# Strided sparse attention with a squared-ReLU feed-forward: v and w_in loads regrouped, v asked for later, and the seven-product form of the second matmul from the third block on

## The chip, the cores and the metric

The kernel runs on one core of one Trainium2 chip. The metric is the device time of one execution in microseconds (us), as the median of several runs; lower is better.

## What is computed

Two stages follow each other. Eight batches of eight heads go through a masked attention over 576 positions of 64 elements: the first four heads see the last 32 positions ("local"), the other four see positions at a distance that is a multiple of 32 ("strided"). The result, 4,608 tokens of 512 elements, goes through a feed-forward of width 2,048 with the activation s * relu(h)^2 + b.

```python
scores = scale * np.matmul(q, k.transpose(0, 1, 3, 2))
mask_local = (rel >= 0) & (rel < stride)
mask_strided = (rel >= 0) & (pos[None, :] % stride == pos[:, None] % stride)
attn = softmax(np.where(masks, scores, -1e9))
x = np.matmul(attn, v)            # (B, H, S, D) -> (B*S, H*D)
h = x @ w_in
g = s * (np.maximum(h, 0.0) ** 2) + b
out = g @ w_out
```

## The kernel before

**Work units.** A batch b is cut into four pairs of heads, m = 0 to 3 (0 and 1 local, 2 and 3 strided). `pair_steps` makes the steps of one pair: transposes of q and k (L429 for the local heads of batches 0 and 1, else L437), scores (L557; in batch 0 the mask is added by L554), exponentials on ACT (L575), a mask multiplication on DVE (L583), the product with v (L614, "AV"), the scaling by the reciprocal of the row sum (L629, then L640 on DVE or L635 on ACT), and a transpose of x into `xT` (L662). From some batch on, transposes of q, k and x are made by DMA on SP's queue instead: local k from batch 4, local q from batch 6, strided q and k from batch 3, local x from batch 2 and strided x in batches 4 to 6, the latter through DRAM (L685 writes, L689 reads back).

The feed-forward works on nine blocks T of 512 tokens. `ff1` (L907, "F1") makes h = x w_in in 16 column groups of four matmuls; ACT takes the ReLU out of PSUM (L934) and DVE or ACT squares it (L944, L942). `ff2` (L965, "F2") makes the second product for blocks 0 to 2: 64 matmuls of 512 columns each. `ff2_seven` makes it for blocks 3 to 8 as seven products in place of eight: 7 x 16 = 112 matmuls of 256 columns (L875), with sums of the activations (L747), differences of w_out's quarters (`w_mix`, L769, made once) and additions as the results leave PSUM (L794, L806, L817). The constant `SEVEN` is the first such block.

**What sets the order.** A planner (`Plan`) runs while the kernel is built. It keeps a clock of its own, an assumed cost for each step and an assumed delay for each result, and writes down one order per engine; on the chip every engine works its list in that order and waits on semaphores. `post` hands in work that is not PE's, with a cost per engine that may do it ("A" ACT, "V" DVE, "P" POOL, "D", "X", "Y" transfers on SP's queue); `flush` places it. `LAT` is the delay that is added after a cost, so an entry "D" is how long a DMA transpose is taken to need. `landing(cost)` is when a load on POOL's queue is taken to have landed. The main loop takes a step of the attention or a step of F1 or F2, whichever is due, and where nothing is ready in the head of the kernel, `keep_running` puts in a filler matmul (L1201).

**The loads.** Nearly all loads are issued by POOL. In the head: q and k of batch 0 in halves (L284), the strided q, k and v (L311), then, behind a copy that waits for qs, w_in in three pieces of 512, 512 and 1,024 columns (L328, in `weights_in`), then in `second` batch 1's q and k (L296), its v in four transfers, one a head (L316, rows of 64 elements), its strided v, w_out in four pieces (L334). Batch 0's local v comes through SP's queue in fp32 (L252, `stage_v`), into a part of w_out's tile, and POOL casts it. `rows_before` copies the 32 rows of v ahead of each band, `cast_v` casts strided v. Later batches: `fetch_qk(b + 2)` waits on POOL for batch b + 1's strided k transposes (copies into `gate`, L1036); `fetch_v(b + 2)` is posted when the last AV of batch b is placed.

In the built program POOL's transfers use eight semaphores in turn, and each transfer waits until the one eight before it has landed.

Of the kernel before, what the change touches and what calls it, by code (L numbers as in the profile page):

```python
# [15 lines left out]
class Plan:  # L16
# [7 lines left out]
    LAT = {"A": 70.0, "V": 70.0, "P": 70.0, "D": 12000.0, "X": 7000.0, "Y": 12000.0}  # L24
# [92 lines left out]
class Step:  # L117
    def __init__(self, fn, ns, needs=(), group=None, keys=(), posts=(), after=None):
        self.fn, self.ns, self.needs, self.group = fn, ns, needs, group
        self.keys, self.posts, self.after = keys, posts, after  # L120
# [3 lines left out]
def kernel(  # L124
# [32 lines left out]
    for p in range(SQ):  # L157
        for c in range(SQ):
# [30 lines left out]
               for i, n in enumerate((512, 512, 1024))]  # L189
# [21 lines left out]
    def x_free(b):  # L211
# [22 lines left out]
    vl_stage = w_out_sb.rearrange("p f m -> p (f m)").bitcast(FP32)[:, 0:NL].rearrange(  # L234
        "p (h t d) -> p h t d", h=4, d=D)
# [34 lines left out]
    for tl in p_bufs[False]:  # L270
        nc.vector.memset(tl[:, 16 * SQ:], 0.0)

# [40 lines left out]
    def load_vl(b):  # L313
        vl = v_loc[b % NV]
        for h in range(4):
            nc.gpsimd.dma_start(out=vl[LPAD:128, h, :, 0:D], in_=v_band(b, h))  # L316
# [8 lines left out]
    def load_w_in():  # L325
        wv = moe_w_in.rearrange("(c p) f -> p c f", p=128)
        for i, at in enumerate((0, 512, 1024)):
# [42 lines left out]
    def rows_before(b, mm, key):  # L370
# [3 lines left out]
        src = vl_stage[:, :, :, 0:D] if b == 0 else vl[:, :, :, 0:D]  # L374
# [3 lines left out]
        plan.post([key], {"P": 800.0} if b == 0 else {"A": 700.0, "V": 350.0}, g, [("in", "vl", b, mm)])  # L378
# [30 lines left out]
    def pair_steps(b, m):  # L409
# [10 lines left out]
        def trans(name, j, group):  # L420
            alone = loc and b < HEAD_T

            def f():
                if j == 0:
                    st["p" + name] = bank(group).bitcast(FP16)[:, 0:S]
                if alone:
                    for e in range(2):
# [12 lines left out]
            s = Step(f, 70 if alone else 35, needs=[("in", name + sfx, b, mm)],  # L440
                     group=group if j == 0 else None)
            if j == nt - 1:
# [35 lines left out]
        x_by_dma = b >= 2 if loc else XS_DMA <= b < B - 1  # L478
# [128 lines left out]
        def av(e, j, group):  # L607
# [13 lines left out]
            if j % per == per - 1:  # L621
# [10 lines left out]
                def mu(eng):  # L632
                    if eng == "A":
                        for i in range(per):
# [12 lines left out]
                                                 **({"A": 225.0 * per} if b == 0 else {})}, mu,  # L647
# [67 lines left out]
    SEVEN = 3  # L715
# [45 lines left out]
    def mix_post():  # L761
# [3 lines left out]
        jobs = ((3, wr[1], wr[0]), (1, wr[0], wl[0]), (2, wr[1], w_mix[1]), (4, wl[1], w_mix[2]))  # L765
        before = [("F2", SEVEN - 1)]
        for i, x, y in jobs:
            plan.post(before, {"V": 1250.0},
                      lambda eng, i=i, x=x, y=y: nc.vector.tensor_tensor(  # L769
                          out=w_mix[i], in0=x, in1=y, op=ALU.subtract), [("w_mix", i)])  # L770
            before = [("w_mix", i)]
# [125 lines left out]
    def ff1(T, ft, ct, group, cts=(0, 1, 2, 3), early=False):  # L897
        tok0 = T * PS
        def f():
# [6 lines left out]
            for lo, hi in ((0, n), (n, PS))[:1 + (n < PS)]:  # L906
                nc.tensor.matmul(  # L907
                    out=gts["h", T, ft][:, lo:hi],
                    lhsT=w_in_sb[min(ft // 4, 2)][:, ct].rearrange(
                        "p (c x l) -> p c l x", x=128, l=4)[:, max(ft // 4 - 2, 0), ft % 4],  # L910
# [111 lines left out]
    def landing(cost):  # L1022
# [4 lines left out]
        return ring + (6000.0 if plan.t > 60000.0 else 600.0)  # L1027
# [4 lines left out]
    def fetch_qk(b):  # L1032
# [6 lines left out]
        for name in ("q", "k"):  # L1039
# [3 lines left out]
            if b < HEAD_T:  # L1043
                arrive(both(name + "l", b), landing(1500))
                continue
            plan.done["raw", name, b] = landing(1700 if b > 1 else 1450)
            for mm in range(2):
                pair_post(b, name, mm, ("raw", name, b))
        for name in ("qs", "ks"):
            arrive(both(name, b), landing(2000 if b > 1 else 1750))  # L1050

    def fetch_v(b):
        load_vl(b)
# [9 lines left out]
    def early_v(b):  # L1063
# [3 lines left out]
        plan.done["raw", "v", False, b] = landing(1800)  # L1067
# [5 lines left out]
    def after_landing(i, src):  # L1073
# [3 lines left out]
    load_qk(0)  # L1077
    early_v(0)
    plan.free["P"] = 7100.0
    plan.free["V"] = 6500.0  # L1080
    AT = {"ql0": 5700.0, "kl0": 6800.0, "ql1": 7900.0, "kl1": 8900.0, "qs": 10100.0,
          "ks": 11600.0, "vs": 13600.0, "vl0": 7100.0, "vl1": 14700.0}
# [6 lines left out]
    stage_v(range(2, 4))  # L1089
# [3 lines left out]
    def weights_in(eng):  # L1093
# [4 lines left out]
        ring = 15300.0  # L1098
        for keys, cost in ([0], 2700), ([1], 2500), ([2, 3], 5000):
            arrive([("w_in", c) for c in keys], landing(cost))  # L1100

    for mm, at in (0, AT["vl0"]), (1, AT["vl1"]):
        plan.done["raw", "v", True, 0, mm] = at
        cast_v(0, True, mm, ("raw", "v", True, 0, mm))
# [7 lines left out]
    def second(eng):  # L1112
# [3 lines left out]
        plan.done["raw", "vl", 1] = landing(3200)  # L1116
# [5 lines left out]
    plan.post(both("vl", 0) + both("vs", 0) + [("w",)], {"P": 14000.0}, second, [("free",)])  # L1122
# [169 lines left out]
```

## Time and profile before

| | |
|---|---|
| median of 3 runs | 305.25 us (304.46 to 308.44) |
| the profiled execution: time, span | 306.2 us, 304.4 us |
| PE busy | 296.4 us (97%) |
| DVE, ACT, POOL busy | 216.6 (71%), 183.9 (60%), 99.3 us (33%) |
| POOL's DMA queue | 57,232 packets, 18.08 MB, 60.1% of 16 engines' span |
| SP's DMA queue | 43,562 packets, 18.78 MB, 33.3% |
| F1, 512 columns (L907) | 440 matmuls, 379 ns each |
| F2, 512 columns (L965) | 192 matmuls, 379 ns each |
| seven-product F2, 256 columns (L875) | 273 ns each |
| granted TensorE clock | 1.000 |

The span runs from the first to the last instruction of the profiled execution. A matmul's duration in the profile is longer than the distance from one start to the next, since matmuls are pipelined; for sums over a list of matmuls the distance is used. A slice of the busy rows is a fortieth of the span, 7.6 us.

### The profile page before, as it was taken

The numbers are of one execution on the slowest core, as the hardware profiler recorded it, in microseconds if no ns is written. First come the engines' busy times: TensorE is split into PE (matmuls) and PEld (weight loads), VectorE is DVE, ScalarE is ACT, GpSimd is POOL, SyncE is SP. The second block draws the span as 40 slices with busy tenths as digits, with TensorE's granted clock in tenths as the row PEclk, the third lists the DMA queues.
The fourth block names the chain that finished last, engine by engine and source line by source line (L and its number), as shares of the span: only waits on it lengthen the run. The fifth ranks groups of instructions, "written<-read, shape, count | busy, mean of one in ns | idle before, by whom it ended". The sixth has DMA issues, their size and how long they took to land.

```text
span 304.4 us, 6800 instructions
## 1 busy us (share of the span) xinstructions
PE 296.4 (97%) x2674; PEld 205.8 (68%) x2674; DVE 216.6 (71%) x474; ACT 183.9 (60%) x330; POOL 99.3 (33%) x146
## 2 busy tenths in 40 slices
PE   8998999999999999999999999999999999999995
PEld 3764655666555568767567776778888666766784
DVE  6665897698966688737997698777765366737563
ACT  2966963898747677478585946695725445445300
POOL 8771753930961095029502961200000000000000
PEclk9999999999999999999999999999999999999999
DMA  8999999999999699999999999944010200300123
GB/s 136 183 201 202 137 213 190 179 198 149 83 160 165 98 100 149 132 186 147 142 153 172 142 160 159 155 105 131 14 37 34 72 34 0 106 0 2 69 82 126
DMA packets 100826, 37.29 MB, mean 122 GB/s; under 512 B 80907, under 2 KB 97803, under 8 KB 100795
## 3 DMA queue, kind: packets, MB, share of 16 engines
q0 software_dynamic: 57232, 18.08, 60.1%
q1 hardware_dynamic: 43562, 18.78, 33.3%
q8 instruction: 21, 0.34, 0.5%
q14 instruction: 11, 0.08, 0.1%
HBM read 36.86 MB, written 10.32 MB: 155 GB/s over the span
## 4 chain that ended last, share of the span: by engine, by line
PE 83%; DMA 8%; DVE 3%; POOL 3%; issue 1%; ACT 1%; POOLq 0%
PE ps_f L907 36%; PE ps_f L875 20%; PE ps_f L965 12%; DMA kl<-in_k_dram 5%; PE ps_s L557 3%; PE ps_a L614 3%; DMA vs<-in_v_dram 2%; PE ps_s L875 2%; DMA xT<-x_dram 1%; PE ps_t L875 1%; PE ps_s L965 1%; PE ps_t L614 1%; PE ps_t L662 1%; PE ps_t L437 1%; PE ps_f L437 1%
## 5 line engine op out<-in xcount | busy, mean ns | idle before, releaser
L907 PE MATMUL ps_f<-xT,w_in_sb 128*128 128x512 f16 (+4 forms) x696 | 148.1, 340 | 0.0
L934 ACT ACTIVATE u<-ps_f 128x512 f16<-128x512 f32 x137 | 80.8, 595 | 72.6 <-PE ps_f L907 69.9
L907 PEld LDWEIGHTS <-w_in_sb 128*128 128x128 f16 x704 | 71.7, 113 | 33.1 <-DMA w_in_sb<-in_moe_w_in_dram 0.5
L875 PEld LDWEIGHTS <-gT 128*128 128x128 f16 x512 | 49.0, 98 | 12.5 <-issue 0.4
L965 PE MATMUL ps_f<-w_out_sb,gT 128*128 128x512 f16 x176 | 47.6, 379 | 0.0
L875 PE MATMUL ps_f<-w_out_sb,gT 128*128 128x256 f16 x312 | 44.2, 273 | 0.3 <-DVE o L806 0.3
L944 DVE TENSOR_TENSOR gT<-u 128x1024 f16<-128x1024 f16 x46 | 32.1, 697 | 15.1 <-ACT u L934 14.4
L942 ACT ACTIVATE gT<-u 128x1024 f16<-128x1024 f16 x26 | 27.5, 1057 | 0.7
L640 DVE TENSOR_TENSOR x_nat<-ps_a,rec 72x256 f16<-72x256 f32 (+1 forms) x55 | 25.3, 459 | 0.9
L316 POOL DMA_DIRECT2D v_loc<-in_v_dram x28 | 20.7, 759 | 14.3 <-DMA w_in_sb<-in_moe_w_in_dram 6.0
L965 PEld LDWEIGHTS <-gT 128*128 128x128 f16 x192 | 17.0, 98 | 11.1
L575 ACT ACTIVATE p_str<-ps_s 72x432 f16<-72x432 f32 (+1 forms) x45 | 20.1, 481 | 4.7 <-PE ps_s L557 4.6
L575 ACT ACTIVATE p_loc<-ps_s 128x384 f16<-128x384 f32 x46 | 20.8, 494 | 2.2 <-PE ps_s L557 1.8
L614 PEld LDWEIGHTS <-p_str 72*128 72x128 f16 x256 | 15.3, 98 | 7.3 <-issue 0.4
L747 DVE TENSOR_TENSOR gT<-gT 128x1024 f16<-128x1024 f16 x28 | 18.5, 683 | 1.4 <-ACT gT L942 1.3
L875 PE MATMUL ps_f<-w_mix,gT 128*128 128x256 f16 x144 | 19.3, 273 | 0.0
L875 PEld LDWEIGHTS <-S 128*128 128x128 f16 x160 | 15.5, 98 | 3.7
L629 DVE RECIPROCAL rec<-ps_a 72x4 f32<-72x4 f32 (+1 forms) x55 | 9.7, 177 | 11.2 <-PE ps_a L614 11.0
L321 POOL DMA_DIRECT2D v_str<-in_v_dram x16 | 13.0, 816 | 9.6 <-PE ps_f L907 5.6
L583 DVE TENSOR_TENSOR p_loc<-p_loc,masks 128x1152 f16<-128x1152 f16 x14 | 10.5, 750 | 7.6 <-ACT p_loc L575 7.4
L875 PE MATMUL ps_f<-w_mix,S 128*128 128x256 f16 x96 | 13.4, 273 | 0.0
L976 DVE SCALAR_TENSOR_TENSOR o<-ps_f,s_sb,bcs 128x512 f32<-128x512 f32 x11 | 8.2, 749 | 6.4 <-PE ps_f L965 6.2
(162 smaller groups left out, 413.2 us busy)
## 6 DMA issues: line engine op xcount, KB each, us to landing
out_dram<-o SPq DMA_DIRECT2D x34, 256.0 KB, 3.4
w_out_sb<-in_moe_w_out_dram POOLq DMA_DIRECT2D x4, 512.0 KB, 9.4
v_loc<-in_v_dram POOLq DMA_DIRECT2D x28, 72.0 KB, 8.5
qs<-in_q_dram POOLq DMA_DIRECT2D x6, 288.0 KB, 6.6
ks<-in_k_dram POOLq DMA_DIRECT2D x6, 288.0 KB, 8.0
ql<-in_q_dram POOLq DMA_DIRECT2D x5, 288.0 KB, 9.7
kl<-in_k_dram POOLq DMA_DIRECT2D x16, 72.0 KB, 3.8
v_str<-in_v_dram POOLq DMA_DIRECT2D x16, 72.0 KB, 9.9
```

The costliest lines, as they stand in the source:

```text
L316: nc.gpsimd.dma_start(out=vl[LPAD:128, h, :, 0:D], in_=v_band(b, h))
L321: nc.gpsimd.dma_start(out=vs[:, h, :, 0:D], in_=v[b, 4 + h].rearrange("(p j) d -> p j d", j=ST))
L575: nc.scalar.activation(out=st["pw", g][0:nk, 0:2 * n * nq], in_=st["s", g][0:nk, 0:2 * n * nq], func=AF.Exp, scale=scale)
L614: nc.tensor.matmul(out=st["a"][:, j % per, :], lhsT=st["pw", g][0:nk, i * nq:i * nq + WIDE], rhs=vt[0:nk, 2 * mm + e, j, :])
L640: nc.vector.tensor_tensor(out=st["x"][:, j0:j0 + per, 64 * e:64 * e + 64], in0=st["pa", e, j][0:nq, 0:per, 0:D], in1=st["rec", e, j][0:nq, ...
L747: nc.vector.tensor_tensor(out=at(out), in0=at(x), in1=at(y), op=op)
L875: nc.tensor.matmul(out=gts[name, T, t][:, 0] if halves else gts[name, T][:, t], lhsT=lhs(k, t), rhs=rhs(k), start=fresh and k == 0 and (ha ...
L907: nc.tensor.matmul(out=gts["h", T, ft][:, lo:hi], lhsT=w_in_sb[min(ft // 4, 2)][:, ct].rearrange("p (c x l) -> p c l x", x=128, l=4)[:, ma ...
L934: nc.scalar.activation(out=u, in_=gts["h", T, ft], func=AF.Relu)
L942: nc.scalar.activation(out=g, in_=u, func=AF.Square)
L944: nc.vector.tensor_tensor(out=g, in0=u, in1=u, op=ALU.mult)
L965: nc.tensor.matmul(out=gts[id_], lhsT=gts[T][:, ft, ts * 128:(ts + 1) * 128], rhs=w_out_sb[:, ft, cols], start=(ft == 0), stop=(ft == NFT ...
```

## The change

- Planner: a DMA transpose is taken to be ready after 8.0 us instead of 12.0 ("D"), a store to DRAM after 6.0 instead of 7.0 ("X"), a transposed read from there after 6.0 instead of 12.0 ("Y"); a late landing 3.0 us after the queue instead of 6.0. Several assumed landing times of the head change. The clock starts at 1.85 us.
- w_in is loaded in four pieces of 512 columns.
- Batch 0's second pair of local heads no longer comes through SP and a cast on POOL, but in one fp16-casting transfer on POOL's queue, ahead of the strided v. Batch 1's local v is one transfer instead of four.
- From batch 2 on `fetch_v(b + 2)` is placed only when all four `xT` of batch b are, and POOL first copies one element of each (`gate`), so it waits for them.
- x scalings may go to ACT in every batch, at 260 ns a group of 64 elements instead of 225 ns in batch 0 alone.
- Strided x of batch 7 goes through DRAM instead of PE's transposes.
- `SEVEN` is 2: block 2 has the seven-product form as well. w_mix 3, 2 and 4 are made after block 0's F2 and the bias sum, w_mix 1, which overwrites a part of w_out, after block 1's F2; w_mix 2 is made from w_mix 3.
- Once a transpose group of batch 0 is begun, its steps go first (`sticky`). Two small ranges of `p_str` are cleared.

```diff
-    LAT = {"A": 70.0, "V": 70.0, "P": 70.0, "D": 12000.0, "X": 7000.0, "Y": 12000.0}
+    LAT = {"A": 70.0, "V": 70.0, "P": 70.0, "D": 8000.0, "X": 6000.0, "Y": 6000.0}
...
-               for i, n in enumerate((512, 512, 1024))]
+               for i, n in enumerate((512, 512, 512, 512))]
...
     def load_vl(b):
         vl = v_loc[b % NV]
+        if b < 2:
+            nc.gpsimd.dma_start(
+                out=vl.rearrange("p h t d -> p (h t) d")[LPAD:128, :, 0:D],
+                in_=v.rearrange("b h (t p) d -> b p (h t) d", p=LQ)[b, :, 0:4 * LT])
+            return
         for h in range(4):
             nc.gpsimd.dma_start(out=vl[LPAD:128, h, :, 0:D], in_=v_band(b, h))
...
-        for i, at in enumerate((0, 512, 1024)):
+        for i, at in enumerate((0, 512, 1024, 1536)):
             nc.gpsimd.dma_start(out=w_in_sb[i], in_=wv[:, :, at:at + w_in_sb[i].shape[2]])
...
-        x_by_dma = b >= 2 if loc else XS_DMA <= b < B - 1
+        x_by_dma = b >= 2 if loc else XS_DMA <= b
...
-                                                 **({"A": 225.0 * per} if b == 0 else {})}, mu,
+                                                 "A": 260.0 * per}, mu,
...
-    SEVEN = 3
+    SEVEN = 2
...
-        jobs = ((3, wr[1], wr[0]), (1, wr[0], wl[0]), (2, wr[1], w_mix[1]), (4, wl[1], w_mix[2]))
-        before = [("F2", SEVEN - 1)]
-        for i, x, y in jobs:
-            plan.post(before, {"V": 1250.0},
+        early = [("bcs",)] + ([("F2", SEVEN - 2)] if SEVEN > 1 else [])
+        jobs = ((3, wr[1], wr[0], ALU.subtract, early), (2, w_mix[3], wl[0], ALU.add, []),
+                (4, wl[1], w_mix[2], ALU.subtract, []),
+                (1, wr[0], wl[0], ALU.subtract, [("F2", SEVEN - 1)]))
...
-        return ring + (6000.0 if plan.t > 60000.0 else 600.0)
+        return ring + (3000.0 if plan.t > 60000.0 else 600.0)
...
+    QUIET = 2
+
     def fetch_v(b):
+        for m in range(4) if b - 2 >= QUIET else ():
+
+            nc.gpsimd.tensor_copy(out=gate[0:1, m:m + 1], in_=x_slot(m, b - 2)[0:1, 0:1])
         load_vl(b)
...
     load_qk(0)
+    nc.gpsimd.dma_start(
+        out=v_loc[0].rearrange("p h t d -> p (h t) d")[LPAD:128, 2 * LT:4 * LT, 0:D],
+        in_=v.rearrange("b h (t p) d -> b p (h t) d", p=LQ)[0, :, 2 * LT:4 * LT])
     early_v(0)
...
-    stage_v(range(2, 4))
...
                 last_av.after = when_all("av", b, lambda b=b: plan.post(
-                    [("fetch", b + 2)] + both("vs", b), {"P": 3600.0}, lambda eng: fetch_v(b + 2),
-                    [("fetch_v", b + 2)]))
+                    [("fetch", b + 2)] + both("vs", b) +
+                    [("xT", b, mk) for mk in range(4) if b >= QUIET],
+                    {"P": 3600.0}, lambda eng: fetch_v(b + 2), [("fetch_v", b + 2)]))
...
+        active.sort(key=lambda p: not att[p][at_i[p]].sticky)
```

## The prediction

> **What bounds the kernel now.** I read the page's busy rows first, then the slices, the waits of PE, the timelines of PE and POOL in the head, and the chain.
>
> ```profile
> PE 296.4 (97%) x2674; PEld 205.8 (68%) x2674; DVE 216.6 (71%) x474; ACT 183.9 (60%) x330; POOL 99.3 (33%) x146
> ...
> PE   8998999999999999999999999999999999999995
> ...
> DMA  8999999999999699999999999944010200300123
> GB/s 136 183 201 202 137 213 190 179 198 149 83 160 165 98 100 149 132 186 147 142 153 172 142 160 159 155 105 131 14 37 34 72 34 0 106 0 2 69 82 126
> ```
>
> PE has no slice under 9 after the fourth, so from about 32 us on the kernel is its list of matmuls: an instruction taken off PE is time won, any other engine matters only if it makes PE wait. In the head PE's digits are 8 and 9 while DMA is at 9 from 8 us to past 100 us. The waits of PE, and its timeline there, say what for:
>
> ```profile
> PE ps_t L429 <- DMA ql<-in_q_dram: 1.4, 1, 1.4
> PE ps_t L429 <- DMA kl<-in_k_dram: 0.6, 1, 0.6
> ```
>
> ```profile
> 23.00 4.05 PE L907 MATMUL ps_f<-xT,w_in_sb 128*128 128x512 f16 x18
> 28.49 0.45 PE L429 MATMUL ps_t<-ident,ql 96*64 96x96 f16 x12 [1.44 <-DMA ql<-in_q_dram]
> 28.77 0.42 PE L429 MATMUL ps_f<-ident,ql 96*64 96x96 f16 x12
> 29.12 1.49 PE L907 MATMUL ps_f<-xT,w_in_sb 128*128 128x512 f16 x6
> 31.23 0.45 PE L429 MATMUL ps_t<-ident,kl 96*64 96x96 f16 x12 [0.62 <-DMA kl<-in_k_dram]
> ```
>
> PE has used up the w_in that it may use (18 F1 matmuls), then waits for batch 1's q and k. Those come when POOL's queue of transfers has come to them; POOL itself waits ahead of each v band:
>
> ```profile
> 22.06 0.75 POOL L316 DMA_DIRECT2D v_loc<-in_v_dram  x1 [1.96 <-DMA w_in_sb<-in_moe_w_in_dram]
> 26.89 0.72 POOL L316 DMA_DIRECT2D v_loc<-in_v_dram  x1 [4.08 <-DMA w_in_sb<-in_moe_w_in_dram]
> 28.73 0.73 POOL L316 DMA_DIRECT2D v_loc<-in_v_dram  x1 [1.11 <-DMA ql<-in_q_dram]
> 31.47 0.72 POOL L316 DMA_DIRECT2D v_loc<-in_v_dram  x1 [2.01 <-DMA kl<-in_k_dram]
> ```
>
> In the built program each POOL transfer waits for the one eight before it (eight semaphores in turn); these four waits fit that exactly. Two rows of the chain give the rates, and the DMA view of single issues two landings:
>
> ```profile
> 44.06 1.73 PE ps_f L965 x8
> ...
> 160.38 2.84 PE ps_f L875 x26
> ```
>
> ```profile
> w_out_sb<-in_moe_w_out_dram POOLq DMA_DIRECT2D x1, 512.0 KB, 6.5
> ```
>
> ```profile
> kT_alt<-kl SPq DMA_TRANSPOSE x1, 9.9
> ```
>
> A 512-column matmul costs 1.73/8 = 0.216 us, a 256-column one 2.84/26 = 0.109. w_out's first piece, issued at 33.63, lands at 33.63 + 6.5 = 40.1; the k transpose issued at 119.88 takes 9.9.
>
> **What the skill says.** "TensorE: Matmul & The Clock Gate", section Back-to-back issue gap: a warm matmul takes N/2.4 + 2.5 ns, so 215.8 and 109.2; the trace has 216 and 109. Halving the width thus costs 2 x 109 - 216 = 2 ns a pair. "DMA: Bandwidth & Descriptors", section Issuing engines are not separate DMA queues: SP's and POOL's transfers run on the same engines and interleave, so moving one from SP to POOL moves no load away. The trace agrees: 202 GB/s at a DMA share of 1.31 in 19.0 to 31.3 us. Same page, Why small descriptors are slow: short pieces pay overhead each. The trace: a window of 256-byte v rows (33.5 to 33.7) moved 78 GB/s, one of q, k and weights (35.5 to 36.4) 211. One v transfer in place of four still has 2,304 such rows, so I expect no faster landing.
>
> **Part 1, PE's list.** T = 2 goes to seven products. Out: 64 matmuls of 512 columns, 64 x 0.216 = 13.8 us. In: 7 x 16 = 112 of 256, 112 x 0.109 = 12.2. Net -1.6. Batch 7's strided x now goes through DRAM: 16 transposes L662 of 72 columns leave PE; four of them take 0.13 us from start to start in the timeline, so 16 x 0.032 = -0.5. Sum **-2.1 us**, certain. The fillers (20 before, 23 narrower ones after) only fill waits and count there.
>
> **Part 2, the head.** Counted in the two built orders. From the first F1 matmul (18.97) to kl's transposes, before has 38 F1; after has 45, and the other work done by then is equal (56 AV, 28 x transposes), because w_in's third piece is now 512 KB and counts as landed at half its way: the old 1 MB piece released POOL at 26.89, its predecessor at 22.06, so the new third lands near 24.5. Now 35 F1 (7.6 us), 12 AV (0.4), 16 transposes (0.5) and fillers (0.3) lie between first F1 and ql: 18.97 + 8.8 + 0.4 of small waits = 28.2, ql at 28.45: wait 0.25, not 1.44. Then 24 transposes and 10 F1, 0.8 + 2.2: 31.45, after kl (31.2): no wait. So seven F1 (1.5 us) more for 0.2 later: 1.3 won at 31 us. But from there to the first L965 lie 7.7 us of work: arrival 31.45 + 7.7 + 0.3 = 39.4, and w_out's first piece lands at 40.1 unless it moves. It cannot move much: bytes ahead of it are the same, and the engines are saturated, so POOL's earlier issue (no four waits of 2.0 + 4.1 + 1.1 + 2.0) only lengthens the queue. PE waits 0.7 there. Before, L965 began at 40.81 with 8 small scores (0.5 us) more done. Won: 40.8 - 40.1 - 0.5 = 0.2; I take **-0.4** (between 0 and -2: the upper end if SP's v rows, now on POOL's queue as fp16, leave w_in sooner). The second v half goes ahead of vs, w_in and all later POOL transfers: bounded by +1 (its rows delay w_in) and -1. POOL loses two casts and two v_str copies (3 us), hidden by w_in's landing at 18.9; the first ql at 5.2 instead of PE's 6.37 is hidden by it too. Without that cover it is worth 1.2.
>
> **Part 3, ACT.** The planner may now give any x scaling to ACT, at 260 ns an element group where it was 225 in batch 0 only. In the built order 76 of them stand on ACT, 12 before.
>
> ```profile
> L635 ACT ACTIVATE x_nat<-ps_f,rec x12: 307/330/362, 17.0 to 19.7; 72x64 f16<-72x64 f32 x12
> ```
>
> 64 x (333 - 260) = 4.7 us of ACT time that the plan doesn't know, in 14 blocks of about 0.3. ACT is at 60%, so most is absorbed; behind a block stands a relu L934 that frees an F1 bank, and PE waits for it if tight. Bounds 0 and +4.7; I take **+0.5**. DVE gains 8 sums (0.68), about 2 us of L794/L806, one add (0.69), loses 14 scalings (about 6): even. The four w_mix operations (1.2 us each) are as many as before and only stand earlier, behind T = 0 and T = 1; the first product that reads one comes 32 matmuls (3.5 us) into T = 2, long after. Four more small memsets (0.1 us each) and the order of batch 0's transposes lie ahead of w_in's landing: nothing.
>
> **Part 4, later v.** From batch 2 on four POOL copies wait for xT(b), then v(b+2). Behind them on POOL: eight v transfers (8 x 0.78), then the next q/k fetch and q copies. For v(4) xT(2) is complete at about 91 us; the gates (0.2 each) and two issues end at 93, landing 8.5 (page), copy 0.4 to 0.7: 102. Its first AV lies 11.7 us of PE work after xT(2)'s last transposes, near 103. Cover 1 us and more; for v(5) to v(7) it is over 5. **0**, at worst 1 each.
>
> **Part 5, plan latencies.** DMA-transposes are now planned at 8.0 us instead of 12.0 and landings at 3 instead of 6 beyond the ring. Batches 4 to 7 are therefore asked of PE up to 18 us earlier. Tightest: k(6,0). Its transpose stands on SP behind xT(5,0), which waits for F1 of T = 3; PE has 9.1 us of work between that issue and the first score. The trace has 4.3 in the median, 7.1 for kT_alt, 9.9 at most. Below nothing is excluded. **+0.2**, bounds 0 and +6.
>
> **Sum.** -2.1 - 0.4 + 0.5 + 0 + 0.2 = -1.8 us on the span: 304.4 to 302.6. The profiled execution took 306.2, 1.8 around the span, so 304.4; it lay 0.95 above the median. Against the median of 305.25: 303.45, say **303.5 us**.
>
> **Rivals.** (a) The head gives more: without SP's rows among POOL's, w_in and w_out land 1 to 2 us sooner, the 0.7 wait goes, the first-ql gain of 1.2 counts. For it: 2 us before w_in SP and POOL loads overlap. Against: the same rows remain. 2.5 us more: 301.0, reaching below 299.15 if the other 4 waits go as well. (b) Slower than before: SP's queue. kT(6,*) and kT(7,*) come late because their SP queue stands behind xT transposes held by F1, and land at 9.9 or more; every us beyond the cover of 9.1 is a PE wait, as PE runs in order. It decides from 2 us of lateness on; 3 to 5 us each in two batches give +6 to +10: about 310. Against: 4.3 median. (c) The change doesn't do what it says: the ACT blocks cost PE all that the seven products save, 2 us: 305.5.
>
> **Chances.** Forecast 0.50 (302 to 305), (a) 0.18, (b) 0.22, (c) 0.10. A third of (a) lies below 299.15 (-2%, about what a measurement of this kernel can tell from no change), a little over half of (b) above 311.35. So faster 0.06, same 0.82, slower 0.12. Range 300.5 to 309.5: it cuts the lower half of (a) and the upper half of (b).
>
> **What would show it.** Right: L875 at 784 matmuls of 109 ns and L965 at 128; PE's wait for kl gone, that for ql under 0.5, a new one of about 0.7 for w_out; PE at 9 from 40 us on. Wrong: PE waits for kT or qT between 125 and 185 us (b), for ACT L635 or L934 (c), for v_loc at 100 us (Part 4), or w_in's first landing away from 18.9 (a).

## The result and the profile after

The changed kernel took 316.06 us in the median of four runs (315.23 to 317.62), against 305.05 for the kernel before: a ratio of 1.0343, 95% interval 1.0258 to 1.0429. It is slower by about 11 us; the forecast of 303.5 and its range up to 309.5 missed it. The profiled execution took 316.18 us with a span of 314.4. (Ratios leave disturbed runs out, so they need not equal the quotient of two medians.)

After's line numbers are those of before plus 7 to 11: scores L565, AV L622, masks L591, ACT's and DVE's x scalings L643 and L648, F1 L918 with its ReLU L944, F2 L975, seven-product F2 L886, row copies L345, local v L323.

The page after: PE's busy time is almost that of before, but its slices now have 8s and 7s between 100 and 205 us, and the granted clock has a 7 in the slice that follows 133 us. DMA stays at 9 about as long as before.

```profile
PE 297.0 (94%) x2709; PEld 211.6 (67%) x2709; DVE 215.8 (69%) x476; ACT 197.5 (63%) x394; POOL 107.2 (34%) x157
...
PE   7989989999999899989997998799999999999994
...
PEclk9999999999999999979999999999999999999998
DMA  8999999996969999999999999923410300200223
```

PE's waits after (us in total, times, longest): the waits for batch 1's ql and kl, which led this list before, are gone. In their place stand three for the strided k transposes, three of over 1 us for DVE's results, and one for the very first ql.

```profile
PE ps_s L565 <- DMA kT<-ks: 6.2, 3, 2.2
PE ps_a L622 <- DVE p_loc L591: 1.6, 1, 1.6
PE ps_f L622 <- DVE p_loc L591: 1.2, 1, 1.2
PE ps_t L670 <- DVE x_nat L648: 1.2, 1, 1.2
PE ps_t L436 <- DMA ql<-in_q_dram: 1.1, 1, 1.1
```

PE's timeline after, in the stretch shown before: 21 F1 matmuls in a row, then ql and kl without a wait.

```profile
24.48 4.70 PE L918 MATMUL ps_f<-xT,w_in_sb 128*128 128x512 f16 x21
29.10 0.45 PE L436 MATMUL ps_t<-ident,ql 96*64 96x96 f16 x12
...
29.73 2.35 PE L918 MATMUL ps_f<-xT,w_in_sb 128*128 128x512 f16 x10
32.01 0.45 PE L436 MATMUL ps_t<-ident,kl 96*64 96x96 f16 x12
```

POOL's timeline after, in the stretch shown before: one v transfer where four stood, and w_out issued at 30.17 instead of 33.63.

```profile
23.93 1.19 POOL L318 DMA_DIRECT2D v_loc<-in_v_dram  x1 [2.31 <-DMA w_in_sb<-in_moe_w_in_dram]
...
30.17 0.55 POOL L341 DMA_DIRECT2D w_out_sb<-in_moe_w_out_dram  x1 [1.70 <-DMA kl<-in_k_dram]
```

The chain after (start, us, what): the two rates are unchanged, 1.08/5 = 0.216 and 2.07/19 = 0.109 us. But the chain now runs through a transpose of 8.93 us, and the seven-product matmuls behind it take 1.71/8 = 0.214 us each, half speed.

```profile
43.83 1.08 PE ps_f L975 x5
...
126.17 8.93 DMA kT<-ks
135.14 0.93 PE ps_s L565 x6
136.08 1.71 PE ps_f L886 x8
...
229.47 2.07 PE ps_f L886 x19
```

The DMA view (median us from issue to landing): the strided k transposes read 8.3 after, where the same row read 2.9 before. These medians stand on few transfers: of the eight transposes the trace has the landing of only two after (8.2 and 8.5) and three before (2.9, 2.9 and 4.4).

```profile
kT<-ks SPq DMA_TRANSPOSE x8, 8.3
```

I took PE's list of matmuls times the start-to-start distances of before (0.216, 0.109, 0.033 and so on) and compared it with the starts in the two traces. Before, the list makes about 290 us, and waits and half clock about 10. After, it is about 287 and 22. So the list became 2.8 us shorter (2.1 of it the steps of Part 1, the rest narrower fillers), and 12 us of waiting and half clock came in. Nearly all of it lies at 107, 133, 165, 194 and 199 us. At 107 us PE waits for an x scaling on DVE, which itself waited 2.28 us for a DMA transpose that reads x.

**At 133 us**, PE's timeline: after the F1 matmuls it waits 2.16 us for the transposed strided k of batch 5, issued by SP at 126.17.

```profile
131.72 1.26 PE L918 MATMUL ps_f<-xT,w_in_sb 128*128 128x192 f16 x10
135.14 0.93 PE L565 MATMUL ps_s<-qD_str,kT 128*72 128x144 f16 x6 [2.16 <-DMA kT<-ks]
135.87 1.92 PE L886 MATMUL ps_f<-w_mix,S 128*128 128x256 f16 x8
```

**At 165 us** PE waits for the strided k of batch 6. SP issues its transposes at 162.46, and PE has done the work ahead of them at 165.45, 3.0 us later; they come 5.1 us after the issue. This lead of the issue over the use is the cover of the transfer: 3.0 us where 5.1 were needed.

```profile
162.46 3.46 SPq L507 DMA_TRANSPOSE kT<-ks  x2
167.60 0.57 PE L565 MATMUL ps_s<-qD_str,kT 128*72 128x144 f16 x6 [2.15 <-DMA kT<-ks]
```

Before, SP issued the same two 1 us earlier, and PE came to them 11.3 us after that, without a wait:

```profile
161.47 3.10 SPq L499 DMA_TRANSPOSE kT<-ks  x2
172.78 0.54 PE L557 MATMUL ps_s<-qD_str,kT 128*72 128x144 f16 x6
```

**At 194 us**, three views tell one story. POOL's timeline: the copies that the change put ahead of v (L1067, the gates) come behind batch 7's q and k; the last of them waits for a transposed read of x, and v goes out at 178.77, where before it went out at 174.19.

```profile
169.09 2.95 POOL L295 DMA_DIRECT2D ql<-in_q_dram  x4
...
178.20 0.18 POOL L1067 COPY gate<-xT 1x1 f16<-1x1 f16 x1 [1.27 <-DMA xT<-x_dram]
178.77 2.92 POOL L323 DMA_DIRECT2D v_loc<-in_v_dram  x4 [0.40 <-PE ps_a L622]
```

DVE's timeline: its copy of v's preceding rows stands ahead of a mask multiplication and waits 3.87 us for the last v transfer, which lands at 193.8.

```profile
193.91 0.33 DVE L345 COPY v_loc<-v_loc 32x640 f16<-32x640 f16 x1 [3.87 <-DMA v_loc<-in_v_dram]
194.26 0.69 DVE L954 TENSOR_TENSOR gT<-u 128x1024 f16<-128x1024 f16 x1
194.87 0.75 DVE L591 TENSOR_TENSOR p_loc<-p_loc,masks 128x1152 f16<-128x1152 f16 x1
```

PE then waits 1.56 us for that mask (L622, the second row of its waits). Before, the same row copy on DVE waited for nothing: v had landed at 184.6, 9 us earlier.

```profile
193.61 0.33 DVE L338 COPY v_loc<-v_loc 32x640 f16<-32x640 f16 x1
```

### The profile page after: what moved, and what is told of

The parts are those of the page before. It is cut to its first block, busy times and chain, and to the rows that moved or that the text cites. A ratio compares the mean times of both kernels' runs of the same rounds, so it can differ in the third digit from the quotient of the medians.

```text
span 314.4 us, 6974 instructions
## 1 busy us (share of the span) xinstructions
PE 297.0 (94%) x2709; PEld 211.6 (67%) x2709; DVE 215.8 (69%) x476; ACT 197.5 (63%) x394; POOL 107.2 (34%) x157
## 4 chain that ended last, share of the span: by engine, by line
PE 77%; DMA 16%; DVE 3%; issue 2%; ACT 1%; SPq 0%; POOL 0%; POOLq 0%; DVEq 0%
PE ps_f L918 31%; PE ps_f L886 20%; PE ps_f L975 7%; DMA kT<-ks 6%; PE ps_s L565 4%; DMA v_loc<-in_v_dram 4%; DMA xT<-x_dram 2%; DMA xT<-x_nat 2%; PE ps_a L622 2%; PE ps_s L886 2%; DMA ql<-in_q_dram 1%; PE ps_t L886 1%; PE ps_s L975 1%; PE ps_t L444 1%; DVE x_nat L648 1%
## 5 line engine op out<-in xcount | busy, mean ns | idle before, releaser
L918 PE MATMUL ps_f<-xT,w_in_sb 128*128 128x512 f16 (+4 forms) x696 | 149.4, 340 | 0.2 <-DVE x_nat L648 0.2
L944 ACT ACTIVATE u<-ps_f 128x512 f16<-128x512 f32 x137 | 80.9, 597 | 58.3 <-PE ps_f L918 57.4
L918 PEld LDWEIGHTS <-w_in_sb 128*128 128x128 f16 x704 | 72.2, 113 | 29.5
L886 PEld LDWEIGHTS <-gT 128*128 128x128 f16 x608 | 57.8, 98 | 13.8 <-ACT gT L952 0.3
L886 PE MATMUL ps_f<-w_out_sb,gT 128*128 128x256 f16 x376 | 53.0, 272 | 0.1
L954 DVE TENSOR_TENSOR gT<-u 128x1024 f16<-128x1024 f16 x45 | 30.7, 685 | 19.4 <-ACT u L944 18.9
L975 PE MATMUL ps_f<-w_out_sb,gT 128*128 128x512 f16 x112 | 29.7, 379 | 0.0
L755 DVE TENSOR_TENSOR gT<-gT 128x1024 f16<-128x1024 f16 x34 | 22.6, 680 | 1.6 <-ACT gT L952 1.4
L886 PE MATMUL ps_f<-w_mix,gT 128*128 128x256 f16 x176 | 22.9, 273 | 0.0
L886 PEld LDWEIGHTS <-S 128*128 128x128 f16 x176 | 17.6, 101 | 4.4
L648 DVE TENSOR_TENSOR x_nat<-ps_a,rec 72x256 f16<-72x256 f32 (+1 forms) x42 | 19.4, 462 | 0.6
L323 POOL DMA_DIRECT2D v_loc<-in_v_dram x24 | 17.6, 745 | 4.9 <-DMA w_out_sb<-in_moe_w_out_dram 3.4
L622 PEld LDWEIGHTS <-p_str 72*128 72x128 f16 x256 | 15.1, 98 | 5.7 <-issue 0.3
L886 PE MATMUL ps_f<-w_mix,S 128*128 128x256 f16 x112 | 17.0, 285 | 0.0
L975 PEld LDWEIGHTS <-gT 128*128 128x128 f16 x128 | 11.5, 98 | 7.8
L345 POOL COPY qD_str<-qT 64x576 f16<-64x576 f16 x6 | 5.2, 864 | 33.5 <-DMA qT<-qs 24.7
L622 PEld LDWEIGHTS <-p_loc 128*128 128x128 f16 x192 | 9.4, 98 | 6.8 <-DVE p_loc L591 3.3
```

Source lines behind the costliest of these rows:

```text
L622: nc.tensor.matmul(out=st["a"][:, j % per, :], lhsT=st["pw", g][0:nk, i * nq:i * nq + WIDE], rhs=vt[0:nk, 2 * mm + e, j, :])
L648: nc.vector.tensor_tensor(out=st["x"][:, j0:j0 + per, 64 * e:64 * e + 64], in0=st["pa", e, j][0:nq, 0:per, 0:D], in1=st["rec", e, j][0:nq, ...
L755: nc.vector.tensor_tensor(out=at(out), in0=at(x), in1=at(y), op=op)
L886: nc.tensor.matmul(out=gts[name, T, t][:, 0] if halves else gts[name, T][:, t], lhsT=lhs(k, t), rhs=rhs(k), start=fresh and k == 0 and (ha ...
L918: nc.tensor.matmul(out=gts["h", T, ft][:, lo:hi], lhsT=w_in_sb[ft // 4][:, ct].rearrange("p (x l) -> p l x", l=4)[:, ft % 4], rhs=xT[ct][: ...
L944: nc.scalar.activation(out=u, in_=gts["h", T, ft], func=AF.Relu)
```

## Experiments

Theory 1: the planner's shorter assumed delays ask PE for transposes and loads before they have landed. Theory 2: the gates hold back later loads. Theory 3: the seven-product block 2 itself. The times of the kernel before beside these runs were 305.7 to 306.2 us.

### Undoing the two parts in the changed kernel

```diff
-    LAT = {... "D": 8000.0, "X": 6000.0, "Y": 6000.0}
+    LAT = {... "D": 12000.0, "X": 7000.0, "Y": 12000.0}
-        return ring + (3000.0 if plan.t > 60000.0 else 600.0)
+        return ring + (6000.0 if plan.t > 60000.0 else 600.0)
```

> The changed kernel with the planner's assumed delays of before: a DMA transpose 12.0 us again, the way through DRAM 7.0 and 12.0, a late landing 6.0 after the queue; the rest of the change stays. Theory 1 (the shorter assumed delays ask PE for strided k of batches 5, 6 and 7 before it has landed): the three waits for kT<-ks (2.33, 2.31 and 2.02 us) and the 1.2 us at half clock behind the first go, so about 308 us. Theory 2 (the copies that hold back the later v hold back everything behind them on POOL): no gate is touched, so at least the v_loc wait of 1.7 and the kT wait of 2.0 in batch 7 stay, 312 us or more. Theory 3 (neither: the seven-product form of block 2 itself costs the time): stays at 316.

Measured: 312.91 us, 1.0217 (1.0145 to 1.0289).

```diff
-    QUIET = 2
+    QUIET = 100
```

> The changed kernel with v of batches 4 to 7 fetched as before (no wait for xT(b), no copies ahead of it); the short assumed delays stay. Theory 1: kT<-ks waits of batches 5 and 6 stay; at most the v_loc wait of 1.7 us and the 2.0 us behind it in batch 7 go, so 312 to 314 us. Theory 2: the transfers of the later batches start earlier and land before they are asked for, all of the 10 us of waits after 100 us shrink, 308 or less. Theory 3: 316.

Measured: 311.78 us, 1.0222 (1.0160 to 1.0283). Then both edits together:

> The changed kernel with both undone: old assumed delays, no gates. What stays of the change is the head's loads, the seven-product form of block 2, ACT scalings in all batches, batch 7's strided x through DRAM. Theories 1 and 2 together: no wait over 1 us after 60 us but those of DVE, about 304.5 (the net of my working of the list, -2.1, against 305.05 and the two DVE waits of 1.3 and the late DMA x wait). Theory 3: over 311.

Measured: 305.43 us, 0.9993 (0.9975 to 1.0011).

The two parts are the whole loss: without both, the time is that of before. Either one left in costs about 7 us (2.2 to 2.3% of 305.7), so they overlap: together 10.6, not 14. Theory 3 falls as the main cause. With both undone no wait of PE for a transfer over 0.84 us is left. Each theory is right about its own waits: with long delays PE no longer waits for k at all, and without the gates one such wait (2.64 us) and one for DVE (2.39) stay.

With the delays long and the gates in, the loss sits at one place. ACT's timeline of that run: two row copies wait for v in turn, 4.38 and 3.49 us, and the ReLU that frees F1's bank stands behind them.

```profile
189.48 0.58 ACT L944 ACTIVATE u<-ps_f 128x512 f16<-128x512 f32 x1
194.44 0.73 ACT L345 COPY v_loc<-v_loc 32x640 f16<-32x640 f16 x1 [4.38 <-DMA v_loc<-in_v_dram]
198.66 0.72 ACT L345 COPY v_loc<-v_loc 32x640 f16<-32x640 f16 x1 [3.49 <-DMA v_loc<-in_v_dram]
199.29 0.58 ACT L944 ACTIVATE u<-ps_f 128x512 f16<-128x512 f32 x1
```

PE's timeline of the same run: it waits 5.87 us for that ReLU, and then its F1 matmuls come every 0.42 us instead of 0.216.

```profile
199.92 1.87 PE L918 MATMUL ps_f<-xT,w_in_sb 128*128 128x512 f16 x4 [5.87 <-ACT u L944]
```

### One part alone on the kernel before

Only the four delays, as in the change:

> The kernel before with only the planner's assumed delays of the change (8.0, 6.0 and 6.0 us; late landing 3.0). Against the changed kernel without gates, which lies 6.4 us over the one with both undone, this asks if the short delays need the rest of the change to do harm. Theory 1 alone: they do not, about 311 us with PE waiting over 2 us for kT<-ks or a transposed q or k twice. Rival (the head, the faster block 2 or batch 7's x through DRAM crowd SP's queue, the delays only show it): 306 to 307.

Measured: 317.9 us, 1.0359 (1.0278 to 1.0439), even more than the whole change. PE's waits in that run, first two rows:

```profile
PE ps_s L557 <- DMA kT<-ks: 3.6, 1, 3.6
PE ps_f L907 <- ACT u L934: 3.0, 1, 3.0
```

The second is once more an engine held by a copy: ACT's copy of batch 6's transposed q waited 6.16 us for its DMA with a ReLU behind it. Theory 1 needs nothing else of the change. The rival (the delays only show a crowded queue) falls. What the delays did can be counted in the cover of the strided k of batches 4 to 7: 12.6, 12.5, 11.3 and 7.8 us in the kernel before, 7.7, 5.4, 6.1 and 5.2 in this run.

Only the gates:

```diff
     def fetch_v(b):
+        for m in range(4) if b - 2 >= QUIET else ():
+            nc.gpsimd.tensor_copy(out=gate[0:1, m:m + 1], in_=x_slot(m, b - 2)[0:1, 0:1])
...
-                    [("fetch", b + 2)] + both("vs", b), {"P": 3600.0}, lambda eng: fetch_v(b + 2),
+                    [("fetch", b + 2)] + both("vs", b) +
+                    [("xT", b, mk) for mk in range(4) if b >= QUIET],
+                    {"P": 3600.0}, lambda eng: fetch_v(b + 2),
```

> The kernel before with only the later v (v of batches 4 to 7 asked for behind xT of two batches earlier, with the copies on POOL). Theory 2 alone: the last v lands 10 to 14 us after its issue at about 182, its row copy stands on ACT or DVE before a relu or a mask, PE waits 5 us or more near 190: about 312. Rival (the gates harm only a kernel that is asked for v early): 306 to 307.

Measured: 305.58 us, 0.9984 (0.9963 to 1.0005). My expectation was wrong, the rival right: alone, the gates cost nothing.

Only `SEVEN = 2` with its order of w_mix:

> The kernel before with the seven-product form from block 2 on and nothing else (with the w_mix order of the change). Theory 1 and 2: the 64 matmuls of 512 columns become 112 of 256, -1.6 us of PE and no new wait: 303.5 us. Theory 3: the change of pace or DVE's sums bring waits: 306 or more.

Measured: 304.81 us, 0.9980 (0.9956 to 1.0004). No loss, but a gain of only 0.6 us (0.2%), where the list gives 1.6, and the interval takes in no gain at all.

The seven-product block and the gates together:

> The kernel before with the seven-product form from block 2 on and the gates, nothing else. Theory A: ACT is not loaded more, so about 305. Theory B: the faster block takes the cover, PE waits for v of batch 7 or behind it: 310 or more.

Measured: 308.6 us, 1.0072 (1.0046 to 1.0098). That is 2.8 us more than the block alone, so Theory A falls; of Theory B the direction is right and not the size (310 or more). Only one wait in that run stands behind the last v: 1.07 us at 195.5, for a ReLU behind a row copy on ACT that waited 2.29. PE's other new waits over 0.9 us are for DVE (1.65 and 0.98), and its clock was at half from 17.6 to 21.1 us. In POOL's queue v of batch 4 goes out at 94.0, as in the changed kernel with long delays (94.1), where the gates alone on the kernel before let it out at 89.9 and without gates it goes at 83 to 84. At 89.9 the later fetches catch up (v of batch 7 at 174.9, before 174.2); at 94 they don't (178.5, and 182.2 in the changed kernel with long delays).

ACT's scalings, a suspect for the late gate, put back in the changed kernel with long delays and gates:

```diff
-                                         "A": 260.0 * per}, mu,
+                                         **({"A": 225.0 * per} if b == 0 else {})}, mu,
```

> The changed kernel with the long assumed delays and with x scalings on ACT only in batch 0, as before; the gates stay. With ACT's scalings this lay at 312.9, the gates alone on the kernel before cost nothing (305.6). Theory A (ACT, busy with scalings, copies xT(2) 4 us later, at 93.4 instead of 89.2, and so opens the gate of v(4) later; every later fetch then starts later): the gates open early again, POOL's first v of batch 7 goes out near 175, about 306. Theory B (it is the faster pace of block 2 and the head that leave the gates no cover): near 312.

Measured: 310.91 us, 1.0137 (1.0091 to 1.0183), v of batch 7 out at 182.3. Theory A falls: the fetches are as late as with the scalings.

### Which delay, and how much of it

In the changed kernel without gates, only the transposes' delays short:

> The changed kernel without gates, the assumed late landing back at 6.0 us, the transposes' delays short (8.0, 6.0, 6.0). Theory 1a (the transposes' delay is what is asked too early): near 311, as with both short, with PE waiting 2 us for kT. Theory 1b (the landing's delay is): 305.5, as with both long.

Measured: 309.97 us, 1.0068 (1.0037 to 1.0099), with times that spread from 305.8 to 313.2, between the two theories. Only the landing short:

> The changed kernel without gates, the transposes' delays back at 12.0, 7.0 and 12.0, the assumed late landing short (3.0 us). Theory 1a: 305.5. Theory 1b: near 311.

Measured: 314.38 us, 1.0287 (1.0213 to 1.0361). The landing, which covers the loads of q, k and v, is the dearer one. The two don't add up: both short gave 1.0222.

Then the kernel before with delays half way, and with longer ones:

```diff
-    LAT = {... "D": 12000.0, "X": 7000.0, "Y": 12000.0}     ... 6000.0 if plan.t
+    LAT = {... "D": 10000.0, "X": 6500.0, "Y": 9000.0}      ... 4500.0 if plan.t
+    LAT = {... "D": 18000.0, "X": 10000.0, "Y": 18000.0}    ... 9000.0 if plan.t
```

> The kernel before with assumed delays half way to the change: 10.0, 6.5 and 9.0 us, late landing 4.5. Cover theory: the last v's row copy, which has 8.8 us of cover with the long delays and waits 2.6 us with the short ones, still has some 2 to 4 us: no transfer wait over 1 us, 305 to 309. Rival (any new plan moves the time, whatever the delays): 310 or more.

Measured: 311.02 us, 1.0115 (1.0038 to 1.0192). It lies between short and own delays, but I expected no transfer wait over 1 us, and there are two causes of that size: 1.3 us for kT, and 2.5 us behind a row copy that sat 3.2 us on ACT. The time is the one that the rival named, and this run doesn't exclude it: its own waits are for transfers, but it may be that almost any other order than the kernel's own costs something.

> The kernel before with longer assumed delays: 18.0, 10.0 and 18.0 us, late landing 9.0. As in the changed kernel with these delays: no wait for a transfer after 60 us, cover of 12 us or more, but attention runs out later, F2's seven-product blocks wait for DVE's evictions 4 to 7 us in all: 309 to 312. If longer is simply safer: 305 to 306.

Measured: 316.79 us, 1.0316 (1.0249 to 1.0384), above what I expected. PE's waits in that run: no transfer after 60 us, but DVE's results at several places. PE's clock was also at half from 155.4 to 162.2 us, around two of these waits. That longer delays cost almost as much as short ones fits the rival of the run before; what shows the short delays' own part is which waits come with them.

```profile
PE ps_a L614 <- DVE x_nat L640: 2.2, 2, 1.6
PE ps_f L875 <- DVE Va L794: 1.5, 3, 0.9
...
PE ps_f L875 <- DVE w_mix L769: 1.3, 1, 1.3
```

The changed kernel, gates and all, with these longer delays:

> The changed kernel, gates and all, with assumed delays longer than before's: 18.0, 10.0 and 18.0 us, late landing 9.0. If the gates cost because the plan leaves too little cover between the fetch and the work that reads it, the 5.9 us behind the last v's row copy go and this lies at 306 to 308 (with 12.0 and 6.0 it was 312.9). If POOL's chain of fetches is the bound, waits only change their place: 312 or more.

Measured: 312.37 us, 1.0203 (1.0183 to 1.0224). Neither reading holds as I wrote it. The waits for transfers do go (v lands at 193.4 and is asked for at 208.2), so the cover was what the gates ate, and POOL's chain is not the bound. But the time does not fall, since other waits come:

```profile
PE ps_f L886 <- DVE Va L805: 3.3, 5, 0.8
PE ps_f L886 <- DVE Vb L805: 1.9, 3, 0.8
```

Attention is asked for later; the seven-product blocks then wait for DVE to empty their banks, eight times 0.25 to 0.84 us.

Side by side, the last v load of all runs: when it is issued, how many of SP's transposes are issued while it is under way, how long it takes to land, when it has landed, and when the engine has come to the second of the two row copies that read it. "Long" delays are those of before, "old ACT" is ACT scalings in batch 0 alone; the last part below has the runs that were not named yet.

| run | v(7) issued | transposes meanwhile | to landing | landed | second copy reached |
|---|---|---|---|---|---|
| changed, longer delays | 184.4 | 4 | 9.0 | 193.4 | 208.4 |
| before, gates | 174.9 | 4 | 9.7 | 184.5 | 192.1 |
| before | 174.2 | 3 | 10.4 | 184.6 | 193.6 |
| before, longer delays | 181.8 | 1 | 10.5 | 192.3 | 204.3 |
| changed, both undone, old ACT | 174.8 | 5 | 11.8 | 186.6 | 190.6 |
| changed, both undone | 172.4 | 5 | 12.6 | 185.0 | 188.7 |
| before, block 2 and batch 7's x, ACT at 333 | 175.7 | 6 | 14.5 | 190.2 | 193.1 |
| before, block 2 | 172.7 | 4 | 14.6 | 187.3 | 189.0 |
| changed | 178.8 | 6 | 15.0 | 193.8 | 190.0 |
| before, head | 176.1 | 6 | 15.1 | 191.2 | 193.3 |
| before, block 2 and gates | 178.5 | 6 | 15.2 | 193.7 | 191.5 |
| before, short delays | 175.1 | 7 | 15.7 | 190.9 | 188.3 |
| changed, no gates | 172.3 | 7 | 16.0 | 188.3 | 187.9 |
| before, half-way delays | 177.3 | 6 | 16.4 | 193.7 | 190.6 |
| changed, long delays | 182.2 | 7 | 16.4 | 198.6 | 195.2 |
| changed, long delays, old ACT | 182.3 | 7 | 16.5 | 198.8 | 196.1 |
| before, block 2 and batch 7's x | 172.7 | 5 | 17.7 | 190.4 | 188.9 |
| before, block 2 and batch 7's x, ACT at 260 | 175.6 | 7 | 18.5 | 194.0 | 193.3 |
| changed, no gates, transposes' delays long | 167.9 | 8 | 19.2 | 187.1 | 183.3 |
| changed, no gates, landing's delay long | 175.7 | 5 | 19.3 | 195.0 | 198.6 |

The same load takes 9.0 to 19.3 us, and the delays don't decide it: with the delays of before and no gates it runs from 10.4 to 18.5. Nor is it shown that the transposes do. Runs with six and more of them lie at 14.5 to 19.2, but those with five at 11.8 to 19.3, block 2 alone has four and 14.6, and a load that takes longer leaves time for more. The Trainium skill says ("DMA: Bandwidth & Descriptors", Issuing engines are not separate DMA queues) that transfers from SP and POOL interleave on the same engines; what that costs v here no run isolates. What the plan does decide is when the copy is reached. In the kernel before that is 9.0 us after the landing; in the changed kernel it is 3.8 us ahead of it, with short delays alone 2.6. Whether PE then loses time depends on what stands behind the copy: with block 2 and batch 7's x alone DVE waits 1.6 us for v, and PE loses 0.5 us there.

### The rest of the change, and a faster version

The head's part alone (loads, assumed landing times, the clock's start, order of batch 0's transposes), made from the changed kernel by undoing all else:

> The kernel before with the head's part alone: one transfer for the second v band and for batch 1's v, w_in in four pieces, the changed landing times and the order of batch 0's transposes. My step said -0.4 (0 to -2): 305.5 against 306. What the runs with these loads suggest: PE's waits up to 41 us sum to 8.75 to 9.9 us where kernels with the old head have 7.5 to 8.4, so +1 to +1.5: about 307.

Measured: 308.8 us, 1.0086 (1.0061 to 1.0111), more than either figure. The changed kernel with long delays, no gates and ACT scalings only in batch 0:

> The changed kernel with long delays, no gates and ACT scalings only in batch 0: head loads, seven-product block 2 and batch 7's x through DRAM remain. If ACT's scalings are what ate the gain of the list (my +0.5, at most 4.7), this falls from 305.4 to 303.5 to 304.5. If the head's loads ate it (the sum of PE's waits to 41 us was 8.75 us in that run, 7.5 in the kernel before), it stays at 305.4.

Measured: 307.75 us, 1.0044 (1.0021 to 1.0067). With the new head and no gates, taking the scalings off ACT made it slower by 0.5%. On the old head, batch 7's x and then the scalings were added to the seven-product block:

```diff
-        x_by_dma = b >= 2 if loc else XS_DMA <= b < B - 1
+        x_by_dma = b >= 2 if loc else XS_DMA <= b
```

> The kernel before with the seven-product form from block 2 on and batch 7's strided x through DRAM: my whole PE list (-1.6 and -0.5) with nothing else changed. If the list counts in full: 303.6 against 305.7. If batch 7's x comes late through DRAM or something else gives the gain back: 305 or more.

Measured: 305.07 us, 0.9979 (0.9959 to 0.9999).

> Seven products from block 2 on, batch 7's x through DRAM and ACT scalings at 260 in all batches; old head, long delays, no gates. My step said ACT costs +0.5 (to 4.7): 305.6 and more against 305.1 without. If ACT's scalings relieve DVE, whose evictions PE waits for (0.7 us at 148 us), as the pair with the new head suggests (305.4 with, 307.7 without): 304 or less, which would beat both kernels.

Measured: 306.77 us, 1.0019 (0.9999 to 1.0039). With 333 a group, as the trace of before shows:

> As the run with ACT scalings at 260, with the cost that the trace shows, 333 a group. If the plan's error of 73 ns a group matters, this is faster than that run by up to 1 us; if ACT has room, the two agree within 0.5 us.

Measured: 305.36 us, 0.9988 (0.9963 to 1.0014). On the old head the scalings do not help; at 333 ACT takes fewer of them (busy 183.9 us against 197.4). The best version is the list alone: seven products from block 2 on and batch 7's x through DRAM, 0.2% below the kernel before and at the edge of what can be told. The block alone has as low a ratio (0.9980), so batch 7's x adds nothing that can be told.

## Why the prediction was wrong

**Part 1, PE's list, -2.1: right as a list.** L886 has 784 matmuls, 0.109 us apart, and L975 128, 0.216 apart. In time it brought less: with nothing else changed, 0.9979 of 306.2 is -0.6 us, 0.03 to 1.3. In that run PE waits 0.7 us just before 149.5 us for DVE's eviction of a seven-product bank (Va), a row that the kernel before doesn't have. In the changed kernel DVE is even, as I had said (215.8 us against 216.6), since ACT takes scalings off it; in the run of the block alone, without that, it is busy for 225.9 us. The rest of the difference isn't settled.

**Part 2, the head, -0.4 (0 to -2): wrong in sign when taken alone.** Alone it costs +2.6 us. In the changed kernel it explains none of the 11 us: up to 60 us PE loses about 10.5 us to waits and half clock where it lost 9.8, and its fillers are 0.7 us shorter. ql's wait went (I had left 0.25), kl's went too, and seven more F1 matmuls lay ahead of kl, as counted. What failed is "the first ql at 5.2 instead of PE's 6.37 is hidden by w_in's landing". PE's timeline at the start of the changed kernel:

```profile
1.06 3.38 PE L1222 MATMUL ps_s<-w_mix 128*128 128x512 f16 x8 [1.06 <-DVE w_mix L257]
5.55 0.69 PE L436 MATMUL ps_t<-ident,ql 96*64 96x96 f16 x12 [1.11 <-DMA ql<-in_q_dram]
6.17 0.82 PE L1222 MATMUL ps_s<-w_mix 128*128 128x256 f16 x4
...
11.46 0.78 PE L1222 MATMUL ps_f<-w_mix 128*128 128x128 f16 x3
12.07 0.23 PE L622 MATMUL ps_f<-v_loc,p_loc 128*128 128x65 f16 x2
```

The fillers end early, PE stands still for 1.1 us, and twelve transposes then take 0.69 us, where before they took 0.45 from 6.37 on: half rate lasts until about 12 us instead of 6 (it shows in the distances of the matmuls, not in the page's clock row). It is no accident of one trace: of the ten kernels with the new head nine have half rate between 8 and 12 us, of the ten with the old head none. The Trainium skill ("TensorE: Matmul & The Clock Gate", What's actually happening) says that full rate follows about 3.4 us of sustained work, and half rate an idle window of about that length. The changed kernel can be read so, with a gap after 3.4 us of fillers. The run of the head alone cannot: there full rate came first and fell to half from 8.4 to 11.8 us, though PE had waited only 1.35 and 0.28 us since its fillers. Batch 0 is thus late: w_in's first piece landed at 18.2 (18.9 before), but the first F1 matmul came at 19.45 (18.97 before). In the run of the head alone it came at 20.16, with w_in there at 17.5. The cover had turned round: w_in waited for PE. Second, 1.2 us went at 41 us (1.7 with the head alone, there behind two row copies and two casts): PE waited for a mask that stood on DVE behind four v casts of 2.34 us in all.

```profile
38.85 2.34 DVE L345 COPY v_str<-vs 72x512 f16<-72x512 f16 x4
...
41.82 0.71 DVE L591 TENSOR_TENSOR p_loc<-p_loc,masks 128x1152 f16<-128x1152 f16 x1
```

Before, DVE made the same casts, but both masks of that batch stood ahead of them (35.96 and 38.45). I had counted what moved between engines, not the order within DVE's list. The w_out wait of 0.7 did not come in the changed kernel, where the first piece landed at 39.1 and not at 40.1; in three other runs with its head it was 0.3 to 1.7.

**Part 3, ACT's scalings, +0.5 (0 to 4.7): not settled.** Their duration was 307 ns, not 333. Their effect has both signs: -1.6 us on the new head without gates (1.0044 to 0.9993), about +2.4 there with the gates (1.0137 to 1.0217, intervals that overlap), +1.2 on the old head (0.9979 to 1.0019). Each such edit gives the planner another order for the whole kernel, and I found no single wait that explains all three. In the trace of the last pair's slower run PE's clock is at half from 18.2 to 21.6 us, which alone is worth up to 1.7 us.

**Part 4, later v, 0: wrong.** Failed is "Cover 1 us and more; for v(5) to v(7) it is over 5". In the changed kernel with long delays the gates cost 6.8 us (1.0217 against 0.9993). I had checked each v against its own first use. But each fetch on POOL stands behind the one before it: v of batch 4 was 10 us late at its gate (94.1, not 84.3), which I had seen, and the lateness was carried on, through SP's transposes and the copies that wait for them: v of batches 4 to 7 goes out 9.8, 8.7, 8.4 and 9.8 us late, the last at 182.2 and not at 172.4. It then takes 16.4 us to land, where I had 8.5, and comes at 198.6. ACT had come to its first row copy at 190.1, so a cover of over 5 us had become a lateness of 8.5, and PE lost 5.87 us and the half clock behind it. In the kernel before the gates alone cost nothing: there v of batch 4 is 6.6 us late, and batch 5 has caught up.

**Part 5, assumed delays, +0.2 (0 to +6): the step that failed most.** Alone it costs +11 us on the kernel before, and 7.0 in the changed one without gates. What failed is "Tightest: k(6,0) ... PE has 9.1 us of work between that issue and the first score". I had priced one transfer, a local k, and it was not the tightest. In the changed kernel PE comes to the strided k of batches 5 to 7 only 6.8, 3.0 and 4.5 us after its issue (12.5, 11.3 and 7.8 before), and it is there after 8.9, 5.1 and 6.3. Two of these covers are near or below even the "4.3 in the median" that I set against 9.1. The landing times were the second fault of the comparison: I took them from the trace of before, and the three that count here came later than that median. Why they did is open; few landings of transposes are in the traces, and the table above shows for v that the delays don't decide it. Third, I had taken only PE as the one that waits. The dearer waits were on ACT and DVE, which work their lists in order: a copy waits for its transfer, and a ReLU or mask behind it holds PE for 1.6 to 5.9 us.

**Rivals and signs.** The named sign of (b), PE waiting for kT between 125 and 185 us, is there, twice. A wait for v_loc came too, but on DVE, at 194 us and not at 100. Of (b)'s mechanism only a part is right. At 133 us the k transposes stood on SP behind two of x that were held for PE, the first of them 1.1 us for F1, and then took 8.9 us themselves. At 165 us they stood behind a store of the result that waited 1.4 us for late DVE work, not behind xT. At 199 us SP had been issuing transposes almost without a break since 174.5. Its 310 is near the 311.8 of the changed kernel without the gates, but the gates were no part of it. Rival (a) did not come. Rival (c) named 305.5, and with delays and gates undone the time is 305.4, but that ACT's blocks eat the gain is not shown (Part 3).

## What to carry to other kernels

An assumed delay in a planner sets how far ahead of its use a transfer is issued: count that cover in the order that the new delays make, for every transfer that they move, and don't take landing times over from another order. Here the kernel's own values beat shorter (+3.6%), half-way (+1.2%) and longer ones (+3.2%); whether these values are good, or any new order costs something, is not separated. A gate on a queue is costed for all that is behind it until the end, not for the first thing that it delays; if lateness isn't caught up within one round, the last round pays. And a small copy that waits for a transfer does not belong, on an engine that works in order, ahead of the operation that frees PE's bank.

## What the runs showed of the hardware that was not expected

After many waits of PE its clock was at half for a while. Of the eleven waits of over 2 us in these runs eight were followed by it (2.16 us at 133 us in the changed kernel, 5.87 with long delays, 2.99 and 3.58 with short delays alone, 2.39 and 2.64 without gates, and two more), three were not (2.15 at 165 us, 2.52 and 3.51 in two other runs). Apart from the start and the end, each such stretch lasted 3.4 or 6.8 us; the one at 133 us left PE 3.2 us at half rate, so about 1.6 us lost. In two runs a stretch of 3.4 us came near 18 us with no wait of over 0.8 us since the first filler. So a wait of over 2 us can cost about 1.4 to 2.4 us more than its length, and not each time; what decides was not tried.
